# Moving a head pair's transposes to token rows one query tile later, and an overflow list's constants behind the routing

## The chip, the cores and the metric

The kernel runs on one core of a Trainium2 chip. A core has five engines that each work through their own list of instructions in order: TensorE (PE in the profile; its weight loads are shown as PEld), VectorE (DVE), ScalarE (ACT), GpSimd (POOL) and SyncE (SP), which here only issues DMA transfers. Matrix products go to PSUM, a small memory that VectorE and ScalarE empty into SBUF, the working memory. The metric is the device time of one execution in microseconds; less is better.

## The reference, cut to what matters

Three parts follow each other. All sizes: 4 batches, 8 heads, 576 tokens, head width 64, model width 512.

```
# 1: attention with a decay from a running sum of s, per batch and head
cum = cumsum(max(s, 0)); bias = min(-(cum[i] - cum[j]), 0)
attn = softmax(q @ k.T / 8 + bias, causal) @ v
x = attn, the 8 heads side by side              # [4, 576, 512]
# 2: a gated dense layer per batch
h = gelu(x @ w_in); u, v = halves of h; v = layernorm(v) * g_ln
v = w_sg @ v (over tokens) + b_sg; x2 = x + (u * v) @ w_out
# 3: a mixture of 8 experts, one expert per token
logits = x2 @ w_gate; local = sigmoid(x2 @ w_local)
e = argmax(logits) where local < 0.5 or at a batch's first token, else the token before's e
out = softmax(logits)[e] * relu(x2 @ w1[e]) @ w2[e]
```

## The kernel before, in words

Nearly every product is made of two or three matmuls on a high part and a low part of its operands (fp32r), so most tiles exist as a pair such as xh and xl.

**Attention.** Heads are taken in order, two to a pair; a pair's 2 x 64 output rows fill the 128 partitions of one tile xf, which has two buffers. A head's queries are cut into five tiles of 128 (the last has 64). For each query tile: a score product (emit_R in batch 1, L496; emit_S, L871), the row's extreme on VectorE (L439), the exponential on ScalarE (L446), its scaling on GpSimd (L450), then transposes of the probabilities (emit_T: L531, copied by L539 and L540). Products with V (emit_PV, L570) come in two parts: the first 256 queries (u = 0) and the other 320 (u = 1). From head 12 on their result is copied by ScalarE (L579) and added by VectorE into xf (L580); before that ScalarE alone writes xf (L582).

**A finished pair.** emit_X(p) does two things with xf. GpSimd splits it into xh and xl (L593, L594), the columns that the dense layer multiplies. TensorE turns it into token rows with five transposes (L599), ScalarE copies these into a staging tile stg (L600, L601; one buffer), and two DMA stores write them to xtok_d in DRAM, from where the output products of the same batch read them back much later.

**Order.** A_steps is a generator: it emits attention work and yields an estimate of its cost. In batch 1 the order is a list (AFTER), run by R_steps and after. In batches 2 to 4 the scores run ahead of the rest by a few query tiles, and after_S does what follows a score: the transposes of its probabilities, after tile 2 the head's product with V for u = 0, after tile 1 the head before's product for u = 1 and, if that head closed a pair, emit_X. merge mixes these steps with those of the dense layer (M_steps) by the yielded costs, until a batch's four pairs are done; take(A, 7) then mixes seven attention steps with the output products of the batch before (O_steps). What is emitted is not yet the order on the engines: a planner, which simulates the engines with durations of its own, draws instructions forward when it believes that their engine would stand idle, and the resulting order of each engine is fixed before the kernel runs. All plain DMAs share SP's one queue, which works in order.

**Routing and overflow.** After a batch's dense layer, route finds each token's expert and its slot. Per token tile VectorE makes three operands from constants (l at L1106, aa at L1108 twice; three buffers each) and TensorE multiplies them into a slot table (L1112). VectorE ends it at L1114 and L1115 (the last entry of dmarks). In the last batch the first layer of expert 0 is already running on TensorE; its sections 0 and 3 are queued behind named routing products (EM). L1241 makes the low part of an expert's weights, once on GpSimd, otherwise on VectorE. emit_olist, emitted in the middle of the experts, builds a list of overflowing blocks; its constants are three rows of numbers from GpSimd (li), cast by VectorE to lf (L1149), and two copies cx (L1151, L1152). behind(x, name) puts x later than the named instruction on the same engine.

Of the kernel before, what the change touches and what calls it, by code (L numbers as in the profile page):

```python
# [24 lines left out]
def f32v(ap):  # L25
    return ap.bitcast(F32)
# [7 lines left out]
def kernel(  # L34
# [19 lines left out]
    PE, ACT, DVE, POOL, SP = nc.tensor, nc.scalar, nc.vector, nc.gpsimd, nc.sync  # L54
# [10 lines left out]
    KD = DM // 128  # L65
# [519 lines left out]
    F4, TA = 8, (1, 3)  # L585

    def emit_X(p):
        b, kt = divmod(p, KD)
        xf = XF.pop(p)
        xh = T(xp, [128, S], F32R, "xh", bufs=6)  # L590
        xl = T(xp, [128, S], F32R, "xl", bufs=6)
        XH[p], XL[p] = xh, xl
        POOL.tensor_scalar(out=xh, in0=xf, scalar1=1.0, scalar2=1.0, op0=ALU.mult, op1=ALU.mult)  # L593
        POOL.tensor_tensor(out=xl, in0=xf, in1=f32v(xh), op=ALU.subtract)  # L594
        pt, pt2 = ps(), ps()
        stg = T(ap_, [128, NQ, 128], F32, "stg")
        for i in range(NQ):
            dst = pt[0:QM[i], 128 * i:128 * i + 128] if i < 4 else pt2[0:QM[i], 0:128]
            PE.transpose(dst, xf[:, 128 * i:128 * i + QM[i]], ident)  # L599
        ACT.copy(out=stg[:, 0:4, :], in_=pt.rearrange("p (i d) -> p i d", d=128))  # L600
        ACT.copy(out=stg[0:QM[4], 4, :], in_=pt2[0:QM[4], 0:128])  # L601
        r0 = b * S
        dma(xtok_d[r0:r0 + 512, 128 * kt:128 * kt + 128].rearrange("(i p) d -> p i d", p=128), stg[:, 0:4, :])
        dma(xtok_d[r0 + 512:r0 + S, 128 * kt:128 * kt + 128], stg[0:QM[4], 4, :])
# [51 lines left out]
    def A_steps(LAG):  # L656
        yield from R_steps()
        fifo = []
        for g in range(2 * PR, NH):
            p, r = divmod(g, 2)  # L660
            for o, i in enumerate((0, 1, 2, 3) if r else (0, 1, 2, 4, 3)):
                if o == 0:
                    for x in when:
                        if when[x] == g:
                            prep_asm(x)
                    if not r:
                        tail_queries(p)
                        prep_cum(p)
                emit_S(g, i) if i < NQ - 1 else emit_tail(p)
                yield 2 * max(107, (128 * i + QM[i]) * 0.42)  # L670
                fifo.append((g, i))
                if r and i == 1:
                    fifo.append((g, NQ - 1))
                if (r, i) in PT2 and p + 1 < NP:
                    prep_T(p + 1, PT2.index((r, i)))
                    if (r, i) == PT2[1] and p + 2 < NP:
                        prep_load(p + 2)
                    yield 600
                for _ in range(LO):
                    if left:  # L680
                        yield from after(*left.pop(0))
                while not left and len(fifo) > LAG:
                    yield from after_S(*fifo.pop(0))
        for x in fifo:
            yield from after_S(*x)
        emit_PV(NH - 1, 1)
        yield 1230
        emit_X(NP - 1)
        done_x[0] += 1
        yield 600  # L690

# [3 lines left out]
    def after_S(g, i):  # L695
        emit_T(g, i)
        yield 110 * (i + 1)
        if i == 2:
            emit_PV(g, 0)
            yield 860  # L700
        if i == 1 and g > 2 * PR:
            emit_PV(g - 1, 1)
            yield 1230
            if g % 2 == 0:
                emit_X((g - 1) // 2)
                done_x[0] += 1
                yield 600
        if i == 1 and g + 2 < NH:
            prep_V(g + 2)

# [5 lines left out]
        (6, ("T04", "P10")),  # L716
        (7, ("P01", "T12", "T13", "V0")),
        (8, ("T14",)),
        (9, ("P11", "V1", "X")),
    ]  # L720

    def after(p, x):
        if x == "X":
            emit_X(p)
            done_x[0] += 1
            yield 600
            return
        g = 2 * p + int(x[1])
        if x[0] == "T":
            emit_T(g, int(x[2]))  # L730
            yield 110 * (int(x[2]) + 1)
        elif x[0] == "P":
            emit_PV(g, int(x[2]))
            yield (860, 1230)[int(x[2])]
        elif g + 2 < NH:
            prep_V(g + 2)
# [400 lines left out]
    def emit_olist(pool, after):  # L1137

        nb = NBLK - CAP
        dma(ids_d, ids)  # L1140
        li = T(pool, [1, 384], I32, "li")
        lf = T(pool, [1, 384], F32, "lf")
        r = T(pool, [128, 48], F32, "ol")
        x = POOL.iota(li[0:1, 0:NL], pattern=[[0, E], [128, nb]], base=128 * CAP, channel_multiplier=0)
        behind(x, after)
        POOL.iota(li[0:1, 128:128 + NL], pattern=[[1, E], [0, nb]], base=0, channel_multiplier=0)
        POOL.iota(li[0:1, 256:256 + NL], pattern=[[NBLK, E], [1, nb]], base=CAP, channel_multiplier=0)
        for a in range(3):
            DVE.tensor_copy(out=lf[0:1, 128 * a:128 * a + NL], in_=li[0:1, 128 * a:128 * a + NL])  # L1149
        cx = T(pool, [128, 2, E, nb], BF16, "cx")  # L1150
        behind(DVE.tensor_copy(out=cx[:, 0], in_=carry.unsqueeze(2).to_broadcast([128, E, nb])), dmarks[-1].ins.name)  # L1151
        DVE.tensor_copy(out=cx[:, 1], in_=pad.unsqueeze(2).to_broadcast([128, E, nb]))  # L1152
        p1 = rs()
        for a in range(3):
            PE.matmul(p1[0:NL, a:a + 1], lhsT=lf[0:1, 128 * a:128 * a + NL], rhs=ident[0:1, 0:1], start=True, stop=True)
        for z in range(2):
            PE.matmul(p1[0:NL, 3:4], lhsT=cx[:, z].rearrange("p e b -> p (e b)"), rhs=onesb[:, 0:1], start=(z == 0), stop=(z == 1))
        DVE.tensor_copy(out=r[0:NL, 0:4], in_=p1[0:NL, 0:4])
        fb = T(pool, [128, 1], BF16, "fb")
        DVE.tensor_tensor(out=r[0:NL, 4:5], in0=r[0:NL, 3:4], in1=r[0:NL, 0:1], op=ALU.is_gt)  # L1160
        DVE.tensor_copy(out=fb[0:NL], in_=r[0:NL, 4:5])
        p2 = rs()
        PE.matmul(p2[0:NL, 0:1], lhsT=ltri[0:NL, 0:NL], rhs=fb[0:NL], start=True, stop=True)
        DVE.tensor_copy(out=r[0:NL, 5:6], in_=p2[0:NL, 0:1])
        DVE.tensor_scalar(out=r[0:NL, 16:16 + NOV], in0=io128[0:NL, 0:NOV], scalar1=r[0:NL, 5:6], scalar2=r[0:NL, 4:5], op0=ALU.is_equal, op1=ALU.mult)
        p3 = rs()
        for a in range(2):
            PE.matmul(p3[0:1, NOV * a:NOV * a + NOV], lhsT=r[0:NL, 1 + a:2 + a], rhs=r[0:NL, 16:16 + NOV], start=True, stop=True)
        PE.matmul(p3[0:1, 2 * NOV:2 * NOV + 1], lhsT=fb[0:NL], rhs=onesb[0:NL, 0:1], start=True, stop=True)
        DVE.tensor_copy(out=olist, in_=p3[0:1, 0:2 * NOV + 1])  # L1170
# [372 lines left out]
```

## Time and profile before

| | |
|---|---|
| median of 3 runs | 828.35 us (828.02 to 830.55) |
| the profiled execution | 832.37 us |
| its span, first to last instruction | 830.1 us |
| TensorE matmuls in flight | 785.8 us, 95% |
| TensorE weight loads | 675.5 us, 81% |
| VectorE, ScalarE, GpSimd busy | 510.2, 436.0, 337.4 us |
| mean granted TensorE clock | 0.985 |

The profile is of one execution. A row of its timeline gives the start and length in us, the engine, the line of the kernel, the operation, written tile <- read tiles, the shape and the number of instructions merged in the row; in square brackets stands how long the engine stood idle before the row and what ended that. A row's length runs from its first instruction's start to its last one's end, and instructions of one engine can overlap by some tens of ns.

### The profile page before, as it was taken

The page shows a single profiled execution, that of the slowest core. Times are in us where ns is not written, and L with a number is a line of the kernel's source. Part 1 is how long each engine was busy: PE and PEld are TensorE (multiplying, and loading weights), DVE is VectorE, ACT ScalarE, POOL GpSimd, SP SyncE. Part 2 cuts the span into 40 slices and gives each one's busy share as a digit, 9 for nine tenths or more (in the row PEclk, how much of TensorE's full clock was granted, in tenths as well). Part 3 has the DMA queues.
Part 4 walks back from the last instruction along what each step waited for, and adds up shares of the span by engine and source line. Part 5 has one row for each costly group of instructions (what it writes and reads, how often), then busy time and mean ns, then how long its engine had stood idle before and what let it go on. Part 6 is the DMA issues. An engine that isn't in the chain of part 4 may idle for free. (4 is left out here: it accounts for less than half of the span.)

```text
span 830.1 us, 14670 instructions
## 1 busy us (share of the span) xinstructions
PE 785.8 (95%) x4832; PEld 675.5 (81%) x4832; DVE 510.2 (61%) x1469; ACT 436.0 (53%) x1040; POOL 337.4 (41%) x614
## 2 busy tenths in 40 slices
PE   9887989899999999999999999989999999999995
PEld 5565877698789799789797778778988989899894
DVE  6787567685776789676884577664644445443420
ACT  6776567675547786246873254144544444444410
POOL 6787436575625578325684010060031220313101
PEclk9999999999999999989999999999999999999998
DMA  8568599845787575768442842153664444635401
GB/s 189 140 188 229 145 267 263 216 145 119 159 254 200 121 219 128 193 199 197 97 155 79 279 143 109 58 191 128 164 212 144 137 165 129 200 113 174 128 4 36
DMA packets 118041, 133.06 MB, mean 160 GB/s; under 512 B 69603, under 2 KB 83043, under 8 KB 117963
## 3 DMA queue, kind: packets, MB, share of 16 engines
q1 hardware_dynamic: 114123, 122.61, 53.6%
q0 software_dynamic: 3840, 9.48, 3.2%
q8 instruction: 40, 0.66, 0.3%
q14 instruction: 38, 0.31, 0.1%
HBM read 90.99 MB, written 22.95 MB: 137 GB/s over the span
## 5 line engine op out<-in xcount | busy, mean ns | idle before, releaser
L1241 DVE TENSOR_TENSOR wp<-wraw,wp 128x1024 fp32r<-128x1024 f32 x63 | 76.6, 1224 | 95.8 <-ACT wp L1240 91.3
L871 PE MATMUL ps<-wp,hT 128*128 128x512 f32 x528 | 123.0, 392 | 0.0
L871 PE MATMUL ps<-xT,wp 128*128 128x384 f32 x672 | 119.1, 336 | 0.0
L871 PEld LDWEIGHTS ps<-xT,wp 128*128 128x128 f32 x672 | 117.3, 188 | 0.7
L871 PEld LDWEIGHTS ps<-wp,hT 128*128 128x128 f32 x528 | 98.6, 188 | 21.1
L1297 POOL DMA_INDIRECT out_dram<-y,ids x24 | 29.4, 1224 | 212.3 <-ACT y L1296 175.0
L1240 ACT CAST wp<-wraw 128x1024 fp32r<-128x1024 f32 x64 | 66.5, 1049 | 62.6 <-DMA wraw<-in_moe_w_dram 56.0
L446 ACT ACTIVATE E<-E,negm 128x128 f32<-128x128 f32 (+4 forms) x136 | 79.4, 585 | 34.3 <-DVE negm L439 30.6
L450 POOL TENSOR_SCALAR E<-E,lsum 128x128 f32<-128x128 f32 (+4 forms) x136 | 77.8, 575 | 37.1 <-DVE lsum L448 28.3
L570 PE MATMUL ps<-et,vv 128*128 128x320 f32 (+9 forms) x476 | 82.5, 314 | 8.5 <-DVE et L537 5.2
L570 PEld LDWEIGHTS ps<-et,vv 128*128 128x128 f32 (+1 forms) x476 | 65.7, 173 | 22.8 <-DVE et L537 6.2
L439 DVE CUSTOM_DVE_ANT_0 E<-ps,zmask 128x128 f32<-128x128 f32 (+4 forms) x136 | 63.5, 471 | 17.9 <-PE ps L871 14.6
L447 POOL TENSOR_SCALAR lsum<-lsum 128x1 f32<-128x1 f32 (+1 forms) x128 | 31.2, 244 | 104.6 <-ACT E L446 88.3
L531 PE MATMUL ps<-ident,E 128*128 128x128 f32 (+1 forms) x452 | 67.6, 262 | 4.6 <-POOL E L450 1.6
L539 ACT CAST et<-ps 128x384 fp32r<-128x384 f32 (+3 forms) x120 | 50.2, 427 | 37.2 <-PE ps L531 35.3
L871 PE MATMUL ps<-wsg,vg 128*128 128x288 f32 x448 | 67.7, 302 | 0.8 <-DVE g L880 0.8
L871 PE MATMUL ps<-xh,w 128*128 128x288 f32 x256 | 59.3, 309 | 4.6 <-DVE wsg L857 2.9
L871 PEld LDWEIGHTS ps<-wsg,vg 128*128 128x128 f32 x448 | 62.0, 191 | 1.4 <-DVE g L880 1.0
L531 PEld LDWEIGHTS ps<-ident,E 128*128 128x128 f32 (+1 forms) x452 | 47.4, 140 | 16.5 <-issue 4.6
L540 DVE TENSOR_TENSOR et<-ps,et 128x384 fp32r<-128x384 f32 (+3 forms) x120 | 57.0, 481 | 4.6 <-ACT et L539 4.1
L871 PE MATMUL ps<-w,vg 128*128 128x512 f32 (+1 forms) x216 | 55.4, 400 | 0.0
L1285 DVE SCALAR_TENSOR_TENSOR hT<-ps,hT 128x384 fp32r<-128x384 f32 x56 | 30.3, 554 | 40.2 <-ACT hT L1284 40.0
(312 smaller groups left out, 1569.9 us busy)
## 6 DMA issues: line engine op xcount, KB each, us to landing
wraw<-in_moe_w_dram SPq DMA_DIRECT2D x64, 512.0 KB
qk<-qk SPq DMA_DIRECT2D x24, 432.0 KB
w<-wv_d SPq DMA_DIRECT2D x16, 512.0 KB
w<-wo_d SPq DMA_DIRECT2D x16, 512.0 KB
qk<-qk SPq DMA_DIRECT2D x24, 288.0 KB
w<-wu_d SPq DMA_DIRECT2D x12, 512.0 KB
nq<-in_q_dram SPq DMA_DIRECT2D x30, 144.0 KB
nk<-in_k_dram SPq DMA_DIRECT2D x30, 144.0 KB
```

Of the source, the lines that this page charges most:

```text
L439: hred[g] = DVE.tensor_tensor_reduce(out=e[:, a:z], in0=pt[:, 0:z - a], in1=zmask[:, m0:m0 + z - a], scale=-1.0, scalar=BIG if hi == 0 els ...
L446: ACT.activation(out=x, in_=x, func=ACTF.Exp, scale=-1.0, bias=nm, accum_out=l[:, z:z + 1])
L447: POOL.tensor_scalar(out=l, in0=l, scalar1=1e-9, scalar2=0.0, op0=ALU.add, op1=ALU.add)
L450: POOL.tensor_scalar(out=x, in0=x, scalar1=l[:, z:z + 1], scalar2=1.0, op0=ALU.mult, op1=ALU.mult)
L531: PE.transpose(pt[:, j * M:(j + 1) * M], e[h, 128 * j:128 * (j + 1)], ident[h, h])
L539: ACT.copy(out=dst[0], in_=src)
L540: DVE.tensor_tensor(out=dst[1], in0=src, in1=f32v(dst[0]), op=ALU.subtract)
L570: PE.matmul(x, lhsT=l, rhs=rhs if g >= F4 else f32v(rhs), start=(j == 0 and n_ == 0), stop=(j == js[-1] and n_ == len(ms) - 1),)
L871: ms = [PE.matmul(pt, lhsT=l, rhs=r, start=(first_ and x == 0), stop=(last_ and x == n - 1)) for x, (l, r) in enumerate(pairs)]
L1240: c = ACT.copy(out=w[:, 0, :], in_=r)
L1241: a = (POOL if (e, j) == (0, KD) else DVE).tensor_tensor(out=w[:, 1, :], in0=r, in1=f32v(w[:, 0, :]), op=ALU.subtract)
L1285: DVE.scalar_tensor_tensor(out=ht[:, 1, f, 0:w_], in0=pt[:, 0:w_], scalar=0.0, in1=f32v(ht[:, 0, f, 0:w_]), op0=ALU.max, op1=ALU.subtract)
```

## The change

In batches 2 to 4 the second half of emit_X (transposes, copies, stores) becomes a step of its own, emit_Y, which is emitted one query tile later: after the next head's tile 2 and its product with V for u = 0. In batch 1 X and Y follow each other in the list as before, but as two entries; the entries of pair 3 that are left over are worked off three to a step, so its Y comes one step later. The last pair's Y follows its X directly. The yields are divided into 50 and 550. In emit_olist, the three casts and the second copy on VectorE are put behind the last routing instruction.

```diff
--- before.py
+++ after.py
@@ -585,13 +585,16 @@
     F4, TA = 8, (1, 3)
 
     def emit_X(p):
-        b, kt = divmod(p, KD)
-        xf = XF.pop(p)
+        xf = XF[p]
         xh = T(xp, [128, S], F32R, "xh", bufs=6)
         xl = T(xp, [128, S], F32R, "xl", bufs=6)
         XH[p], XL[p] = xh, xl
         POOL.tensor_scalar(out=xh, in0=xf, scalar1=1.0, scalar2=1.0, op0=ALU.mult, op1=ALU.mult)
         POOL.tensor_tensor(out=xl, in0=xf, in1=f32v(xh), op=ALU.subtract)
+
+    def emit_Y(p):
+        b, kt = divmod(p, KD)
+        xf = XF.pop(p)
         pt, pt2 = ps(), ps()
         stg = T(ap_, [128, NQ, 128], F32, "stg")
         for i in range(NQ):
@@ -686,6 +689,7 @@
         emit_PV(NH - 1, 1)
         yield 1230
         emit_X(NP - 1)
+        emit_Y(NP - 1)
         done_x[0] += 1
         yield 600
 
@@ -698,13 +702,16 @@
         if i == 2:
             emit_PV(g, 0)
             yield 860
+            if g % 2 == 0 and g > 2 * PR:
+                emit_Y((g - 1) // 2)
+                yield 550
         if i == 1 and g > 2 * PR:
             emit_PV(g - 1, 1)
             yield 1230
             if g % 2 == 0:
                 emit_X((g - 1) // 2)
                 done_x[0] += 1
-                yield 600
+                yield 50
         if i == 1 and g + 2 < NH:
             prep_V(g + 2)
 
@@ -716,14 +723,18 @@
         (6, ("T04", "P10")),
         (7, ("P01", "T12", "T13", "V0")),
         (8, ("T14",)),
-        (9, ("P11", "V1", "X")),
+        (9, ("P11", "V1", "X", "Y")),
     ]
 
     def after(p, x):
         if x == "X":
             emit_X(p)
             done_x[0] += 1
-            yield 600
+            yield 50
+            return
+        if x == "Y":
+            emit_Y(p)
+            yield 550
             return
         g = 2 * p + int(x[1])
         if x[0] == "T":
@@ -1146,10 +1157,10 @@
         POOL.iota(li[0:1, 128:128 + NL], pattern=[[1, E], [0, nb]], base=0, channel_multiplier=0)
         POOL.iota(li[0:1, 256:256 + NL], pattern=[[NBLK, E], [1, nb]], base=CAP, channel_multiplier=0)
         for a in range(3):
-            DVE.tensor_copy(out=lf[0:1, 128 * a:128 * a + NL], in_=li[0:1, 128 * a:128 * a + NL])
+            behind(DVE.tensor_copy(out=lf[0:1, 128 * a:128 * a + NL], in_=li[0:1, 128 * a:128 * a + NL]), dmarks[-1].ins.name)
         cx = T(pool, [128, 2, E, nb], BF16, "cx")
         behind(DVE.tensor_copy(out=cx[:, 0], in_=carry.unsqueeze(2).to_broadcast([128, E, nb])), dmarks[-1].ins.name)
-        DVE.tensor_copy(out=cx[:, 1], in_=pad.unsqueeze(2).to_broadcast([128, E, nb]))
+        behind(DVE.tensor_copy(out=cx[:, 1], in_=pad.unsqueeze(2).to_broadcast([128, E, nb])), dmarks[-1].ins.name)
         p1 = rs()
         for a in range(3):
             PE.matmul(p1[0:NL, a:a + 1], lhsT=lf[0:1, 128 * a:128 * a + NL], rhs=ident[0:1, 0:1], start=True, stop=True)
```

## Rows read from the trace of the kernel before

**Rows 1.** Busy time by stretch: stretch, length, each engine's busy us, clock, DMA share, GB/s

```profile
366.00:450.00 84.00, 80.34 (x568) 72.54 (x568) 62.49 (x194) 57.97 (x156) 52.69 (x103) 0.99 0.46 120
530.00:545.00 15.00, 11.97 (x79) 8.87 (x78) 10.97 (x47) 2.93 (x5) 3.10 (x3) 1.00 0.20 62
545.00:830.00 285.00, 275.45 (x1441) 249.19 (x1440) 119.24 (x164) 116.16 (x179) 58.11 (x49) 0.99 0.44 139
```

**Rows 2.** TensorE's waits: line, waited for, us in total, times, longest

```profile
PE rt L1112 <- DVE aa L1108: 3.6, 3, 2.7
PE ps L599 <- DVE xf L580: 3.6, 4, 1.3
```

**Rows 3.** Timeline of TensorE at pair 9, and at the last pair

```profile
283.87 0.44 PE L599 MATMUL ps<-ident,xf 128*128 128x128 f32 x2
285.06 0.55 PE L599 MATMUL ps<-ident,xf 128*128 128x128 f32 x3 [0.76 <-DVE xf L580]
285.36 0.49 PE L871 MATMUL ps<-qk 128*128 128x256 f32 x2
285.69 0.49 PE L531 MATMUL ps<-ident,E 128*128 128x128 f32 x3
285.94 0.65 PE L570 MATMUL ps<-et,vv 128*128 128x256 f32 x4
...
447.49 0.55 PE L599 MATMUL ps<-ident,xf 128*128 128x128 f32 x3 [1.28 <-DVE xf L580]
```

**Rows 4.** Timeline of ScalarE, VectorE and GpSimd at pair 9

```profile
284.07 0.42 ACT L579 COPY xc<-ps 64x320 f32<-64x320 f32 x1 [0.65 <-PE ps L570]
...
284.52 0.48 DVE L580 TENSOR_TENSOR xf<-ps,xc 64x320 f32<-64x320 f32 x1 [0.38 <-ACT xc L579]
...
283.41 1.05 POOL L450 TENSOR_SCALAR E<-E,lsum 128x512 f32<-128x512 f32 x2
```

**Rows 5.** Timeline of TensorE in the last batch's routing

```profile
540.53 0.54 PE L1112 MATMUL rt<-aa,l 128*128 128x288 bf16 x3
543.76 0.28 PE L1112 MATMUL rt<-aa,l 128*128 128x288 bf16 x1 [2.69 <-DVE aa L1108]
544.38 0.28 PE L1112 MATMUL rt<-aa,l 64*128 64x288 bf16 x1 [0.34 <-DVE aa L1108]
```

**Rows 6.** Timeline of VectorE and GpSimd in the same stretch

```profile
540.46 0.22 DVE L1152 COPY cx<-pad 128x120 bf16<-128x120 bf16 x1
540.59 2.51 DVE L1149 CAST lf<-li 1x120 f32<-1x120 int32 x2
543.02 0.24 DVE L1106 TENSOR_SCALAR l<-io,cf 128x128 bf16<-128x128 bf16 x1
...
540.30 2.58 POOL L1241 TENSOR_TENSOR wp<-wraw,wp 128x1024 fp32r<-128x1024 f32 x1 [0.47 <-ACT wp L1240]
```

**Rows 7.** Lines 1149 and 1108: ns shortest/median/longest, first and last start

```profile
L1149 DVE CAST lf<-li x3: 201/203/2375, 540.6 to 652.4; 1x120 f32<-1x120 int32 x3
...
L1108 DVE TENSOR_SCALAR aa<-ioc,cf,wtok x40: 299/314/757, 234.0 to 544.0; 128x144 bf16<-128x144 bf16 x40
```

**Rows 8.** Lines 600 and 601, the copies into stg, likewise

```profile
L600 ACT COPY stg<-ps x16: 571/586/590, 40.0 to 448.0; 128x512 f32<-128x512 f32 x16
...
L601 ACT COPY stg<-ps x16: 258/259/268, 40.5 to 448.4; 64x128 f32<-64x128 f32 x16
```

**Rows 9.** Timeline of SP's DMA queue at pair 9

```profile
286.15 0.95 SPq L78 DMA_DIRECT2D xtok_d<-stg  x2
287.19 0.56 SPq L78 DMA_DIRECT2D vr<-in_v_dram  x1
```

**Rows 10.** Timeline of VectorE and GpSimd in batch 2's routing

```profile
361.47 1.03 DVE L1108 TENSOR_SCALAR aa<-ioc,cf,wtok 128x144 bf16<-128x144 bf16 x2
...
361.45 0.72 POOL L429 TENSOR_TENSOR vv<-vr,vv 128x256 fp32r<-128x256 f32 x1
```

**Rows 11.** Busy time by stretch behind the routing, columns as in rows 1

```profile
544.00:548.00 4.00, 3.67 (x20) 3.48 (x20) 3.20 (x9) 1.00 (x2) 2.17 (x2) 0.66 0.44 151
```

## Prediction

> **What bounds the kernel now.** I read the busy time by stretch first [rows 1]. TensorE has matmuls in flight for 80.34 of 84 us where attention and the dense layers run interleaved (366 to 450) and for 275.45 of 285 us in the expert part; VectorE, ScalarE and GpSimd have a quarter or more of those stretches free. So an edit pays only where it takes a wait off TensorE, and a wait taken off another engine is worth nothing by itself. One stretch differs: from 530 to 545, the routing of the last batch, TensorE has only 11.97 of 15 us.
>
> Next I read who made TensorE wait [rows 2]. Two rows belong to this change. The products of the slot table (line 1112) waited 3.6 us in three waits for VectorE, the longest 2.7. The transposes to token rows (line 599) waited 3.6 us in four waits for VectorE's last addition into xf, the longest 1.3. The rest of TensorE's 44 us of idle time (830.1 less 785.8) lies on lines that are not touched. So the direct stake is about 7 us of 830.
>
> Then I read both places in order of time. At pair 9 [rows 3] two transposes, which need only the part of xf that was finished earlier, follow the last product with V at once; the other three start at 285.06, after 0.76 us of nothing. The reason is in the other engines' rows [rows 4]: ScalarE's copy of the product's lower half starts at 284.07 and takes 0.42, VectorE's addition starts at 284.52 and takes 0.48, so xf is complete at 285.00. This in-order wait is what moving the transposes can take away. It is rarer than the code suggests: 16 pairs run the same code, four waits of this kind are recorded [rows 2]. Of their 3.6 us, the 1.28 before 447.49 is the last pair's [rows 3]; the other three (pairs 6, 9 and 13) share 2.3, 0.76 or 0.77 each. At the remaining pairs other matmuls stood in front of the transposes.
>
> At the routing [rows 5, 6], TensorE starts three table products at 540.53, then waits 2.69 for the fourth and 0.34 for the fifth. Between the operands of the third token tile and those of the fourth, VectorE ran one copy for the overflow list (540.46) and two casts of 120 numbers on one partition, 2.51 together. Such a cast takes 201 ns at its fastest and 2375 ns here [rows 7].
>
> **The token rows, part by part.** No instruction is added or removed: per pair five transposes, two copies of 586 and 259 ns [rows 8] and two stores, in another place. The split on GpSimd into xh and xl stays where it was. Eleven pairs (4 to 14) move behind the next head's product with V for its first 256 queries; pair 3 moves by one query tile; pairs 0 to 2 and the last keep their order, so the last pair's 1.28 us stays.
>
> At pair 9 the score matmul (285.36), the transposes of the probabilities (285.69) and four value products (285.94) would come first [rows 3]. They need nothing of xf; GpSimd's scaling of probabilities, two in 1.05 from 283.41, is over at 284.46 [rows 4]. They would fill TensorE from about 284.3 to 285.3, and xf is done at 285.00, before its transposes come up. So a wait of 0.76 goes. From start to start it is a little more: transposes follow each other at 0.14 ((0.55 less 0.27 for one) over two), so the third could have started at 283.87 + 2 x 0.14 = 284.15 and started at 285.06, 0.9 later. Three pairs give 3 x 0.76 = 2.3, at most 3 x 0.9 = 2.7. I take 2.3, the idle time that the rows show. For the other eight pairs I count nothing: no wait is recorded there now.
>
> Cost of the move: the two copies, 0.845 us on ScalarE, now stand among the exponentials and probability copies of the next head. Their cover is ScalarE's free time, 26 of 84 us in the stretch to 450 [rows 1]. With the cover gone each of the 11 pairs would cost up to 0.845, 9.3 in all; I take 0 and keep 9.3 as the far end. The stores go through SP's one queue, in order: at pair 9 it issued them from 286.15 in 0.95 us, with a load of a coming V at 287.19 right behind [rows 9]. After the change that load is ahead of them, and nobody waits for a token row before the output products of its batch, a whole stretch later. I take 0; were a load of V late by a store's wait, it would have a head's time in hand. xf has two buffers, and the one of pair p is written again only for pair p+2, so no wait comes from there. In the two stretches where seven attention steps are mixed with an output product, the moved transposes are now one of the seven, and one step of the next head slides into the following stretch. That costs nothing as long as TensorE bounds both.
>
> **The overflow constants.** The casts and the copy may now start only behind the finished slot table. One cast already ran at 652 us [rows 7]. Gone from the routing are the copy and two casts. Read naively this returns the 2.2 us (2375 less 201 ns) that the first cast lost. But why did it take 2375 ns? GpSimd ran a subtraction over 128x1024 from 540.30 for 2.58, to 542.88 [rows 6], and the cast, from 540.59, is over at 542.96, just behind it. The table's own operands are VectorE instructions of one input from SBUF as well: at 361.47 one of line 1108 took 757 ns against a median of 314, and a GpSimd subtraction ran from 361.45 to 362.17 [rows 7, 10]. So whatever of this kind stands next in VectorE's queue stays until GpSimd is done, and after the change that is the operand itself (line 1106, which ran at 543.02 [rows 6]). Having three buffers, it also waits for the first table product, which starts at 540.53 [rows 5], behind GpSimd's start. Then the operand ends at about 542.96, where the first cast ended, and its successor starts where the second cast did, at about 542.9 instead of 543.2: 0.3 us gained. The two ends are therefore 0.3 if the operand is held and 2.2 if it is not. I take 0.3, the row of 757 ns being the nearest.
>
> The Trainium skill's page "SBUF — State Buffer" (section "Who interferes with whom") says that VectorE's copies, casts and tensor_scalar operations in a two-port form and GpSimd's operations hold one pair of ports in turn, the later one blocked until the earlier ends. By that rule the operands are blocked as the casts were, and the term is 0.3; without it, 2.2. The 757 ns agree with the rule; that line 1106 itself is blocked no row here shows.
>
> The moved casts land behind 545, where VectorE is busy for 119 of 285 us [rows 1]; should GpSimd hold one again for 2.2, the evictions queued behind it are late by that, which the seven PSUM buffers cover (without them, TensorE waits those 2.2).
>
> **Sum.** 2.3 + 0.3 = 2.6. The profiled execution took 832.37 (span 830.10 and 2.27 around it), so it would take 829.8. It lies 4.0 above the median of the runs; the same difference from 828.35 gives 825.7. With one of the three pairs not repaid it is 1.8, with the start-to-start figure 3.0: the likeliest case's own range is 825.3 to 826.6.
>
> **Rivals.**
> *The routing is freed entirely.* If VectorE's operands pass GpSimd, the routing returns 2.2, and perhaps the clock as well: behind the two waits the granted clock was 0.66 from 544 to 548 [rows 11], part of the time at 1.2 instead of 2.4 GHz, a loss of 4 x 0.34 = 1.4. With the pairs 2.3 + 2.2 + 1.4 = 5.9, so 822.4. For it: nothing but the casts is seen to be held for so long. Against: the 757 ns. Chance 0.15.
>
> *Nothing comes of it.* The wait moves: TensorE reaches the next tile's probabilities 0.76 earlier and waits there for GpSimd or ScalarE, and the routing is held by GpSimd. Gain 0 to 0.5, so 828.1. For it: the slack at pair 9 is thin (probabilities done at 284.46, wanted at about 284.5). Against: only matmuls that are ready stand ahead at pair 9. Chance 0.22.
>
> *Slower: the copies on ScalarE.* Each pair's 0.845 us in front of a next head's exponential or probability copy delays the chain that TensorE waits for. At 6 of 11 pairs it costs 5.1 less the 2.6, 2.5 slower, and from there it decides; at all 11, 9.3 less 2.6 = 6.7. So 830.9 to 835.1. For it: ScalarE is busy for 58 of 84 us there and works in order, and the planner that fixes that order works from its own durations. Against: 26 us are free, and a copy does not wait for xf any more when it comes up. Chance 0.21.
>
> The forecast has the remaining 0.42.
>
> **How the numbers follow.** Runs of this kernel can tell about 0.3%, 2.5 us, from no change. The forecast's 2.6 lies on that bound: I give 0.24 of its 0.42 to faster and 0.18 to no change. Faster: 0.24 + 0.15 + 0.03 of the second rival = 0.42. No change: 0.18 + 0.19 = 0.37. Slower: the third rival, 0.21. The range from 821.5 to 832 leaves out the edge of the freed routing (0.05) and the upper half of the slower case (0.1).
>
> **What would show it.** In the profile after: no wait of line 599 on xf at pairs 6, 9 and 13, and the last pair's still there; the copies of line 600 amid the next head's work; no casts between the table's operands, but one operand of some 2.3 us there while GpSimd subtracts, and TensorE's wait for line 1112 still above 2. The prediction is wrong if that wait falls below 1, if the waits of lines 531 or 570 grow by more than 2 us, or if the order, which is planned anew for the whole kernel, opens a wait of the routing's size at a place that the change does not name.

## The result, and the profile after

The changed kernel takes 821.55 us (median of 19 runs, 815.12 to 829.23) against 830.55 for the kernel before in the same rounds (19 runs, 822.5 to 841.34). The ratio is 0.99, with a 95% interval of 0.9877 to 0.9923: faster by 1.0%, 8.3 us of 830. The forecast was 825.7 with a range of 821.5 to 832. The direction is right and the time is inside the range by 0.05 us, but the gain is some three times the 2.6 us of the sum. That the time is inside is luck: the forecast started from 828.35, and a ratio of 0.99 on that would be 820.1, below the range.

The first lines of the page of the profiled execution after (its time is 822.43, its span 820.6):

```profile
span 820.6 us, 14652 instructions
PE 784.2 (96%) x4832; PEld 674.7 (82%) x4832; DVE 513.1 (63%) x1469; ACT 436.0 (53%) x1040; POOL 334.8 (41%) x614
```

TensorE still has nearly the same work, 784.2 us against 785.8. What went is its idle time: 820.6 less 784.2 is 36.4, where it was 44.3. The kernel is bound as it was, and in these two profiles 7.9 of the 9.5 us by which the spans differ are idle time of TensorE. The waits of TensorE that answer to [rows 2]:

```profile
PE rt L1123 <- DVE aa L1119: 3.1, 4, 2.3
PE ps L602 <- DVE xf L580: 1.3, 1, 1.3
```

Line 1112 is now line 1123, and 599 is 602. Of the four waits for VectorE's xf one is left, 2.3 us are gone. Two more waits of the transposes, 0.40 and 0.95 us at pairs 0 and 1, are for the xf that ScalarE writes there (line 582). They stand in both profiles, and the change keeps the order of these two pairs; the prediction, which says that at the remaining pairs other matmuls stood in front, overlooked them. The timeline of TensorE at pairs 6, 9 and 13 and at the last pair, which answers to [rows 3], shows which:

```profile
196.12 0.73 PE L602 MATMUL ps<-ident,xf 128*128 128x128 f32 x5
...
282.74 0.45 PE L570 MATMUL ps<-et,vv 128*128 128x256 f32 x3
283.03 0.73 PE L602 MATMUL ps<-ident,xf 128*128 128x128 f32 x5
...
398.31 0.73 PE L602 MATMUL ps<-ident,xf 128*128 128x128 f32 x5
...
438.11 0.55 PE L602 MATMUL ps<-ident,xf 128*128 128x128 f32 x3 [1.28 <-DVE xf L580]
```

At pairs 6, 9 and 13 the five transposes are one row of 0.73 us with no bracket behind it. Value products of the next head stand in front of them. The last pair, whose order was kept, still waits its 1.28. The copies into stg now stand amid the next head's work on ScalarE, between its copy of a value product (579) and its copies and exponentials of the probabilities (539, 446):

```profile
283.59 0.37 ACT L579 COPY xc<-ps 64x256 f32<-64x256 f32 x1
283.99 0.59 ACT L603 COPY stg<-ps 128x512 f32<-128x512 f32 x1
284.47 0.26 ACT L604 COPY stg<-ps 64x128 f32<-64x128 f32 x1
284.63 0.43 ACT L539 CAST et<-ps 128x320 fp32r<-128x320 f32 x1
```

They take 0.59 and 0.26, as before [rows 8], and TensorE does not wait longer for the probabilities than before: its waits of line 570 for VectorE's copies (537) are 4.9 us after and 5.2 before, those of line 531 for GpSimd's scaling 1.7 and 1.6.

The timelines of TensorE, VectorE and GpSimd in the last batch's routing answer to [rows 5, 6]:

```profile
531.51 0.54 PE L1123 MATMUL rt<-aa,l 128*128 128x288 bf16 x3
534.31 0.28 PE L1123 MATMUL rt<-aa,l 128*128 128x288 bf16 x1 [2.26 <-DVE aa L1119]
534.93 0.28 PE L1123 MATMUL rt<-aa,l 64*128 64x288 bf16 x1 [0.34 <-DVE aa L1119]
...
530.82 0.25 DVE L1117 TENSOR_SCALAR l<-io,cf 128x128 bf16<-128x128 bf16 x1
531.84 1.96 DVE L1117 TENSOR_SCALAR l<-io,cf 128x128 bf16<-128x128 bf16 x1 [0.33 <-PE rt L1123]
537.20 0.34 DVE L1160 CAST lf<-li 1x120 f32<-1x120 int32 x2
...
531.39 2.36 POOL L1252 TENSOR_TENSOR wp<-wraw,wp 128x1024 fp32r<-128x1024 f32 x1 [0.50 <-ACT wp L1251]
```

The casts have left the routing (two run at 537.20, in 0.34 together). In their place the operand of line 1117 takes 1.96 us, where the same instruction took 0.25 a microsecond earlier. It ends at 533.80, just behind GpSimd's subtraction (531.39 + 2.36 = 533.75). TensorE's waits for operands in the routing go from 2.69 + 0.34 to 2.26 + 0.34.

So both places that the change names behave as forecast, and they give 2.3 + 0.4 us. The profiled spans differ by 9.5. The table of stretches tells where the rest is. It is cut at the same instructions in both kernels: the start of the transposes of pair 2, the end of the product that ranks each batch's tokens (the last with tile u), the last table product, the last matmul. Columns are stretch, length, busy time of TensorE, its weight loads, VectorE, ScalarE, GpSimd, granted clock, DMA share, GB/s. Before:

```profile
76.90:215.90 139.00, 127.80 (x888) 110.68 (x887) 89.11 (x289) 89.06 (x248) 80.06 (x161) 0.96 0.74 193
215.90:333.50 117.60, 115.18 (x809) 102.37 (x808) 92.74 (x324) 78.22 (x218) 70.75 (x153) 1.00 0.70 181
333.50:456.00 122.50, 116.82 (x766) 101.94 (x765) 86.10 (x284) 68.52 (x185) 63.10 (x125) 0.97 0.56 152
...
527.60:544.70 17.10, 14.07 (x86) 10.52 (x87) 12.93 (x58) 3.17 (x6) 3.10 (x3) 1.00 0.19 60
544.70:820.50 275.80, 275.75 (x1442) 249.49 (x1442) 119.54 (x165) 115.47 (x178) 57.13 (x48) 0.99 0.46 143
```

And after:

```profile
78.40:211.40 133.00, 125.68 (x884) 109.75 (x882) 88.99 (x286) 89.09 (x248) 79.20 (x160) 0.95 0.77 201
211.40:327.90 116.50, 115.86 (x812) 103.21 (x812) 94.44 (x326) 77.74 (x218) 70.33 (x152) 1.00 0.71 183
327.90:446.70 118.80, 115.04 (x766) 100.19 (x765) 87.62 (x284) 68.48 (x184) 63.68 (x126) 1.00 0.60 157
...
518.60:535.20 16.60, 14.01 (x86) 10.46 (x86) 12.13 (x55) 3.17 (x6) 2.83 (x3) 1.00 0.18 55
535.20:811.00 275.80, 275.80 (x1443) 249.54 (x1442) 120.05 (x169) 115.31 (x178) 55.78 (x48) 0.99 0.45 144
```

Read the lengths in pairs. Up to pair 2 the order is the same, and after is 1.5 longer there (78.4 to 76.9). The second stretch, with pair 9, is 1.1 shorter and the routing 0.5: what was priced. The expert part has the same 275.80. The third lost 3.7, and the first lost 6.0, though of the waits that the change aims at only pair 6's 0.76 lies in it. The surplus sits there, and the experiments had to tell which of it is the change's.

### The profile page after: what moved, and what is told of

The parts are those of the page before. It is cut to its first block, busy times and chain, and to the rows that moved or that the text cites. A ratio compares the mean times of both kernels' runs of the same rounds, so it can differ in the third digit from the quotient of the medians.

```text
span 820.6 us, 14652 instructions
## 1 busy us (share of the span) xinstructions
PE 784.2 (96%) x4832; PEld 674.7 (82%) x4832; DVE 513.1 (63%) x1469; ACT 436.0 (53%) x1040; POOL 334.8 (41%) x614
```

## The experiments

In what follows a version's "net length" is the time from pair 2's transposes to the last table product with each stretch multiplied by its granted clock. It takes off most of what a stretch at the lower clock level costs in one profiled execution and not in the next. It is worked out from tables like the two above, so it is an estimate. How good it is can be seen up to pair 2, where TensorE's order is the same in all versions: lengths of 76.9, 80.7 and 86.0 us there (before, "constants only", "pair 3 alone") become 76.9, 75.9 and 75.7. It takes off about 1 us too much where the clock was low for long; so lengths as they stand are given beside it where a reading rests on it. Before it is 133.4 + 117.6 + 118.8 + 71.6 + 17.1 = 458.5, and after 126.3 + 116.5 + 118.8 + 71.9 + 16.6 = 450.1: 8.4 less, as much as the runs measure. Each ratio below is to the kernel before in the same rounds, with its 95% interval.

| version | ratio | net length | of it in the first stretch |
|---|---|---|---|
| before | 1 | 458.5 | 133.4 |
| constants only | 1.0012 (0.9978 to 1.0045) | 458.3 | 133.2 |
| the change | 0.9900 (0.9877 to 0.9923) | 450.1 | 126.3 |
| the change, run again | 0.9871 (0.981 to 0.9932) | 450.3 | 127.4 |
| token rows only | 0.9937 (0.9905 to 0.9969) | 449.5 | 126.8 |
| change, eight steps taken | 0.9935 (0.99 to 0.997) | 450.3 | 127.1 |
| accounting only | 0.9972 (0.9943 to 1.0001) | 457.9 | 129.0 |
| move only | 0.9978 (0.9946 to 1.0009) | 457.1 | 132.5 |
| move, 600 and 0 | 0.9931 (0.9902 to 0.996) | 456.6 | 130.3 |
| pairs 3 to 7 | 0.9967 (0.9928 to 1.0006) | 455.6 | 127.2 |
| pairs 8 to 14 | 0.9952 (0.9912 to 0.9992) | 457.6 | 134.2 |
| pair 3 alone | 0.9918 (0.9891 to 0.9945) | 453.1 | 127.1 |
| pairs 4 to 14 | 0.9944 (0.9909 to 0.9979) | 454.7 | 131.1 |
| subtraction on VectorE | 0.9885 (0.982 to 0.995) | 448.3 | 127.7 |

### The two halves apart

Token rows only: the change, with the four constants back where they were.

```diff
-            behind(DVE.tensor_copy(out=lf[...], in_=li[...]), dmarks[-1].ins.name)
+            DVE.tensor_copy(out=lf[...], in_=li[...])
-        behind(DVE.tensor_copy(out=cx[:, 1], ...), dmarks[-1].ins.name)
+        DVE.tensor_copy(out=cx[:, 1], ...)
```

> The token rows moved as in the change, the overflow constants left where they were; TensorE, ScalarE, GpSimd and SP run exactly the changed kernel's order, VectorE all but five instructions of it. If the constants are worth what the profiles show at the routing (waits of line 1112 there 3.03 us before, 2.60 after), this kernel is 0.4 us slower than the full change, ratio to before about 0.990 to 0.991, and the 2.4 us cast is back between the operands. If the constants carry a large part (2.2 us and 1.4 us of clock), the ratio is 0.994 or more.

Measured: 823.84 against 827.83. On TensorE, ScalarE, GpSimd and SP the order is that of the change, and only rows of VectorE differ. The casts are back in the routing and the wait there is again 2.69 + 0.22, against 2.26 + 0.34 in the change. The net length is that of the change. The ratio, 0.9937, lies between what was expected with the constants worth little (0.990 to 0.991) and with a large part (0.994 or more), and its interval reaches into both. So most of the gain belongs to the token rows; whether the constants have a part is seen in the next run.

Constants only: the kernel before, with the opposite edit.

```diff
-            DVE.tensor_copy(out=lf[...], in_=li[...])
+            behind(DVE.tensor_copy(out=lf[...], in_=li[...]), dmarks[-1].ins.name)
-        DVE.tensor_copy(out=cx[:, 1], ...)
+        behind(DVE.tensor_copy(out=cx[:, 1], ...), dmarks[-1].ins.name)
```

> Only the overflow constants behind the routing, the token rows as before. TensorE, ScalarE, GpSimd and SP run exactly the order of the kernel before, VectorE all but these few rows. Theory held operand: line 1106 takes about 2 us under GpSimd's subtraction, the waits of the table products fall from 3.03 to about 2.6 us, the ratio is 0.999 to 1.000. Rival (the casts alone were late): the waits fall below 1, ratio 0.996.

Measured: 828.95 against 829.23, no difference. In the routing the waits are 1.83, 0.33 and 0.33, 2.5 us in all against 3.0 before. Here it is the third tile's operands of line 1108 that are held: the two take 2.73 us from 535.97, beside GpSimd's subtraction from 536.29 for 2.35. TensorE, ScalarE, GpSimd and SP have exactly the order of the kernel before here, which makes its table a second profiled execution of that order. Its first and third stretch:

```profile
80.70:215.20 134.50, 125.26 (x888) 108.22 (x886) 89.25 (x289) 89.02 (x248) 80.20 (x161) 0.99 0.76 199
332.80:452.50 119.70, 114.81 (x766) 99.81 (x765) 85.85 (x284) 67.74 (x184) 63.12 (x125) 1.00 0.57 155
```

The third stretch takes 119.70 at clock 1.00, where the profile of before had 122.50 at 0.97. So of the 3.7 us by which the change seemed shorter there, 2.8 belong to that one execution of the kernel before: a wait of 1.43 us at 359.58 for VectorE's g and a clock of 0.57 from 360 to 368. Neither is in this run. What remains is 119.7 to 118.8, 0.9: pair 13's wait. The net length of the first stretch, on the other hand, is the same in both executions (133.2 and 133.4), and the change takes 6 to 7 off it. TensorE's order in that stretch is one and the same in three of the versions (before, "constants only", "pairs 8 to 14") and in six others (the change twice, "token rows only", "eight steps taken", "pairs 3 to 7", "subtraction on VectorE"). Without the clock taken off, the three take 139.0, 134.5 and 136.9 us there and the six 130.6 to 133.0: 5.1 less on average.

### The routing: who holds the operand

The change, with the one subtraction that GpSimd does for the first expert's weights given to VectorE.

```diff
-        a = (POOL if (e, j) == (0, KD) else DVE).tensor_tensor(out=w[:, 1, :], in0=r, in1=f32v(w[:, 0, :]), op=ALU.subtract)
-        if (0, KD) < (e, j) < (1, KD):
+        a = DVE.tensor_tensor(out=w[:, 1, :], in0=r, in1=f32v(w[:, 0, :]), op=ALU.subtract)
+        if (0, KD) <= (e, j) < (1, KD):
```

> The changed kernel, but the low part of expert 0's first second-layer weights is made by VectorE behind the finished slot table instead of by GpSimd in the middle of the routing. Theory held operand (line 1117 took 1.96 us because GpSimd's subtraction of 2.36 was running): the operand takes 0.25, TensorE's wait for the fourth table product falls from 2.26 below 0.5, the routing is 1.7 to 2.2 us shorter, the low clock behind it may go too (1.7 more), ratio to before 0.986 to 0.988. Rival (the operand waits for something else, such as the weights' transfer or a buffer): the wait stays above 1.5 and the ratio is that of the change.

Measured: 820.08, ratio 0.9885; the change in the same rounds 819.46 and 0.9871. TensorE and VectorE in the routing:

```profile
531.74 0.28 PE L1123 MATMUL rt<-aa,l 128*128 128x288 bf16 x1 [0.55 <-DVE aa L1119]
...
530.98 0.25 DVE L1117 TENSOR_SCALAR l<-io,cf 128x128 bf16<-128x128 bf16 x1 [0.32 <-PE rt L1123]
533.49 2.36 DVE L1252 TENSOR_TENSOR wp<-wraw,wp 128x1024 fp32r<-128x1024 f32 x2
```

Without GpSimd at work the operand takes its 0.25 again, and the wait of 2.28 that the change has there in the same rounds falls to 0.55. The clock behind it stays up as well: 1.00 from 533 to 537, where the change has 0.57. That settles what holds the operand.

The Trainium skill's page "SBUF — State Buffer" (section "Who interferes with whom") says that GpSimd and a VectorE tensor_scalar in a two-port form hold a shared pair of ports in turn, the later one blocked until the earlier is done. The trace agrees with that rule: 1.96 us beside GpSimd and 0.25 without it.

Whether this version is faster the runs cannot tell: their intervals are 0.6% to either side, some 5 us. The timeline of TensorE tells what became of the gain. This version:

```profile
530.65 0.54 PE L1123 MATMUL rt<-aa,l 128*128 128x288 bf16 x3
...
557.90 1.47 PE L1282 MATMUL ps<-ident,xg 128*128 128x128 f32 x12
559.86 0.73 PE L882 MATMUL ps<-wp,hT 128*128 128x512 f32 x2 [0.49 <-ACT hT L1357]
561.24 3.03 PE L882 MATMUL ps<-wp,hT 128*128 128x512 f32 x12 [0.64 <-DVE hT L1358]
564.10 0.33 PE L882 MATMUL ps<-xT,wp 128*128 128x384 f32 x1
```

And the change in the same rounds:

```profile
529.14 0.54 PE L1123 MATMUL rt<-aa,l 128*128 128x288 bf16 x3
531.95 0.28 PE L1123 MATMUL rt<-aa,l 128*128 128x288 bf16 x1 [2.28 <-DVE aa L1119]
...
559.64 1.47 PE L1282 MATMUL ps<-ident,xg 128*128 128x128 f32 x12
560.87 3.44 PE L882 MATMUL ps<-wp,hT 128*128 128x512 f32 x14
564.15 0.33 PE L882 MATMUL ps<-xT,wp 128*128 128x384 f32 x1
```

This version comes to the routing 1.51 us behind (530.65 to 529.14), because the stretch before it ran at a clock of 0.98 in this execution and at 1.00 in the other. The shorter wait puts it 0.21 ahead (531.74 to 531.95), and the higher clock 1.74 ahead at the transposes of xg (557.90 to 559.64). Then TensorE waits 0.49 and 0.64 for evictions of hT, and at 564.10 the lead is 0.05. In front of these evictions stands a weight tile: ScalarE's cast of it waited 0.31 for its transfer and ran at 558.28 for 1.05, and VectorE's part of it at 559.36 for 1.23. Both spans are 818.2. So of 3.3 us won, 1.7 by the wait and 1.5 by the clock behind it, about 1.7 are lost at hT. The other 1.5 stay, and equal spans hide them only because this execution came late to the routing. It is one execution each, and the ratios neither show nor exclude 1.5 us. The 0.4 of the constants is below what the runs can tell as well, as the run with the constants alone says.

### The move and its accounting

The change says two things to the planner: where the transposes go, and that a step with X takes 50 and one with Y 550 instead of 600 together. These versions take them apart, and try whether one step that slid over a border is what pays. First, everything as in the change, but eight attention steps mixed with an output product instead of seven.

```diff
-            merge(take(A, 7), O_steps(b), 7.0, O_COST)
+            merge(take(A, 8), O_steps(b), 7.0, O_COST)
```

> The full change with eight instead of seven attention steps mixed with each output product, so that these stretches hold the same attention work as before the change. Theory output stretch (the gain of 3.7 us between the second and third routing comes from one attention step sliding out of the stretch where TensorE waited 1.43 us at 359.6 for an output tile's addition): that wait and the low clock behind it return, ratio to before 0.994 or more. Theory merge (the gain is in the mixed stretches): ratio 0.989 to 0.991, as the change.

Measured: 822.92, net length 450.3, as the change, and the wait and the low clock in the third stretch did not come back (118.5 us at a clock of 1.00). The slid step is not the cause. The ratio, 0.9935, is that of "token rows only" in the same rounds.

Accounting only: Y's work done at the end of X, where it was before, with the separate steps kept and empty.

```diff
+        emit_Y0(p)     # at the end of emit_X
-    def emit_Y(p):
+    def emit_Y0(p):
...
+    def emit_Y(p):
+        pass
```

> The transposes, copies and stores stay directly behind the split into xh and xl, as before; only the accounting of the change is kept: 50 at X, and an empty step of 550 where Y would stand; constants as in the change. Theory moved transposes (the gain is the transposes' own place): the waits of line 599 on xf stay (about 2.3 us in three pairs) and the ratio is 0.997 to 1.003. Theory merge (the gain comes from the other interleaving of attention and dense layer that the new steps and yields bring): at least half of the gain without any moved transpose, ratio 0.990 to 0.995.

Measured: 825.74, 0.28% less. There are six waits for VectorE's xf, 4.7 us in all, two more than before. The first stretch is shorter by 4.4, but the second and the third are longer by 2.5 and 4.1; part of the 4.1 are five matmuls that stood in the fourth stretch before (771 against 766), which is 2.3 shorter.

Move only: the transposes moved as in the change, with 600 for X and no step of Y's own. That is so for pairs 4 to 14; pair 3 keeps its two entries in batch 1's list, with 50 and 550, here and in the version behind it.

```diff
-                yield 550
...
-                yield 50
+                yield 600
```

> The transposes, copies and stores moved as in the change for pairs 4 to 14, but with the old accounting: 600 at X and no step for Y, so the mixing counts as before the change; constants as in the change. Theory moved transposes: ratio 0.989 to 0.992, as the change. Theory merge: only the three pairs' waits and the constants are gained, 2.6 us, ratio 0.996 to 0.998.

Measured: 827.37, 0.22% less (1.8 us, near the 2.3 of the pairs, but the interval reaches to no change). Waits for VectorE's xf: the last pair's alone. But among TensorE's waits there is one of 2.1 for VectorE's g, and one that neither the kernel before nor the change has:

```profile
PE ps L881 <- POOL vg L946: 1.6, 1, 1.6
```

And with 600 for X and a step of its own at 0 for Y:

```diff
-                yield 550
+                yield 0
...
-                yield 50
+                yield 600
```

> The change with 600 charged at X and 0 at Y: Y stays a step of its own and counts among the seven, only the charge of 550 comes before the next head's tile instead of behind it. Theory charge (the charge of 550 behind the tile is what shifts the mixing): idle time as with the old accounting, about 22 us, the wait for the output tile's addition is back, ratio 0.996 to 0.998. Theory step (that Y is one of the seven steps): idle time 17 to 18.5 us, ratio 0.989 to 0.993.

Measured: 824.39, 0.69% less, net length 456.6. Only the last pair waits for VectorE's xf, and a wait for GpSimd's vg is there (1.59).

In all of these the waits for xf go or come as the mechanism says. What the version is worth beyond that does not follow them: the same move gives 0.2%, 0.7% or 1.0% with three sets of numbers for the planner, and the intervals of the first and the last do not meet.

### Which pairs

The change again, as it is, for comparison with the three versions of its rounds.

> The changed kernel once more, beside the parts of it on one chip. Both theories: ratio to before 0.988 to 0.992. Its profile against the first one tells how much of a stretch's length is the execution's own (clock, transfers): the order of every engine is the same, so the idle time of TensorE between the second pair's transposes and the last routing should again be near 14.7 us, against 21.9 before.

Measured: 819.46, ratio 0.9871; span 818.2, waits for xf 1.3.

Pairs 3 to 7 moved, the others as before:

```diff
-            if g % 2 == 0 and g > 2 * PR:
+            if g % 2 == 0 and g > 2 * PR and (g - 1) // 2 < 8:
...
+                if not ((g - 1) // 2 < 8):
+                    emit_Y((g - 1) // 2)
...
-                yield 50
+                yield 50 if (g - 1) // 2 < 8 else 600
```

> The change for pairs 3 to 7 alone (they stand in the first mixed stretch and the first output stretch); pairs 8 to 14 as before; constants as in the change. Theory first stretch (most of the gain, 7 us without the clock's share, lies between the second pair's transposes and the first routing): ratio 0.990 to 0.993. Theory pair by pair (0.76 us for each of pairs 6, 9 and 13): only pair 6 and the constants, 1.2 us, ratio 0.998 to 0.999.

Measured: 828.94 against 831.47, ratio 0.9967. Waits for VectorE's xf: 3.3 us in four, all at pairs that were not moved. The first stretch is as short as in the change (127.2), but the second and third are 3.3 and 1.4 longer than its 116.5 and 118.8.

Pairs 8 to 14 moved (the same test with `>= 8`, and pair 3 as before):

> The change for pairs 8 to 14 alone; pairs 3 to 7 as before; constants as in the change. Theory first stretch: what is left is the wait of 1.43 us at 359.6 with the low clock behind it and pairs 9 and 13, at most 5 us where both go, ratio 0.994 to 0.997. Theory pair by pair: 2 x 0.76 and the constants, ratio 0.997 to 0.998.

Measured: 827.3, ratio 0.9952. The first stretch, where nothing is moved, keeps the length of the kernel before (134.2), and pair 6 waits 1.12. The second and third are as short as in the change.

Pair 3 alone (the test with `< 4`):

> Only pair 3's transposes stand one query tile later, as a step of their own in batch 1's list; pairs 4 to 14 as before; constants as in the change. Theory of many small waits (TensorE's idle time between pair 2's transposes and the last routing, 25.0 us before and 16.7 to 17.3 with the change, is made of many places, and each new order of the planner changes several of them): the first mixed stretch loses 1 to 2 us of idle time at the wait of line 857, the three waits on xf stay, ratio 0.996 to 0.999. Theory first stretch (its gain comes from the start of the mixing, which pair 3's move shifts): idle time 20 us or less, ratio 0.993 or less.

Measured: 822.04 against 829.23, ratio 0.9918. Of the two theories on record, the one of many small waits expected 0.996 to 0.999 and missed; the other expected 0.993 or less, and that came. Its profiled execution took 831.32, 9.3 us more than the median; 9.1 of that it lost before pair 2, at a low clock (86.0 us, where before took 76.9), so only the stretches behind are read. Pair 9 keeps its wait, on TensorE's timeline:

```profile
286.87 0.33 PE L602 MATMUL ps<-ident,xf 128*128 128x128 f32 x1 [0.76 <-DVE xf L580]
```

Pair 13 keeps its wait too. The change is 3.0 shorter than this in net length, 1.8 of it in the second stretch and 0.8 in the third, where those two waits lie. The rest of the change's gain is here already, in the first stretch (127.1), with one pair of twelve moved: and pair 3 waited for nothing before.

All but pair 3 (pairs 4 to 14):

```diff
-        (9, ("P11", "V1", "X", "Y")),
+        (9, ("P11", "V1", "X")),
...
+            emit_Y(p)
-            yield 50
+            yield 600
```

> The change without pair 3: its transposes stay with the split; pairs 4 to 14 moved with the new steps and yields; constants as in the change. Theory of many small waits: idle time of TensorE 17 to 19 us, ratio 0.990 to 0.993. Theory first stretch (pair 3's move matters): idle time above 20 us, ratio 0.995 or more.

Measured: 825.62, ratio 0.9944, between the two theories' ranges (0.990 to 0.993, and 0.995 or more). Waits for VectorE's xf: the last pair's alone. The first stretch is 131.1 net, 2.3 less than before; but it had a clock of 1.00 throughout, and as it stands it is as long as the change's own 130.6 to 133.0. So this run does not show that the first stretch needs pair 3's move. The third is that of the change (118.6), but the second is 117.6, that of the kernel before, though pair 9's wait is gone.

## Why the prediction was right, and why its size was not

**The transposes** were right in mechanism and size. 2.3 us of waiting for xf are gone, at the three pairs named, and the last pair's 1.28 stays. In "pair 3 alone", where pairs 9 and 13 are not moved, their 0.76 is still there. The third stretch gives 0.9 for pair 13 (119.7 to 118.8), which is the start-to-start figure. The second gives 1.1, but not by pair 9 alone: TensorE's idle time there falls from 2.4 to 0.6, and four matmuls more lie in it.

**The moved copies** cost nothing that shows: 0.59 and 0.26 us inside ScalarE's free time, with the waits of lines 531 and 570 as before. The rival of the late copies on ScalarE, 830.9 to 835.1, is refuted, and by the same rows the one in which the wait only moves. Nor do the stores show as holding up a load: TensorE's only wait for a load of V is one of 2.1 us in the profiles of both kernels.

**The constants** were right in mechanism and near in size: the operand itself is held, 0.4 us instead of 0.3, and not the 2.2 of the free routing. Giving the subtraction to VectorE shows that GpSimd holds it. The rival of the freed routing, 822.4, came near the result, but not by its mechanism. With the operand freed by that edit, the routing and the clock behind it gave 1.7 + 1.5 us, where the rival had 2.2 + 1.4; what it lacked is that about half is lost again at the evictions of hT.

**The step that failed** is the one that took the rest of TensorE's idle time as lying "on lines that are not touched", and with it the count of nothing for pair 3 and the eight pairs without a wait. The lines are not touched, but the order is: it is planned anew for the whole kernel from the emitted steps and their accounts. Compared place by place in the two traces, with line numbers left out, another instruction stands at about 1160 of TensorE's 4832 places, 700 of VectorE's 1469, 490 of ScalarE's 1040 and 270 of GpSimd's 614. The prediction named this as a way to be wrong, but only as a wait that opens and without a price. Here it closed some. TensorE's waits from 76.9 to 215.9 before:

```profile
PE ps L871 <- DVE wsg L857: 2.9, 1, 2.9
PE ps L570 <- DMA vv<-in_v_dram: 2.1, 1, 2.1
PE ps L871 <- DVE negm L439: 1.2, 2, 1.0
PE ps L599 <- DVE xf L580: 0.8, 1, 0.8
```

The same order once more ("constants only", 80.7 to 215.2):

```profile
PE ps L871 <- DVE wsg L857: 1.4, 1, 1.4
PE ps L871 <- DVE negm L439: 1.2, 2, 1.0
PE ps L599 <- DVE xf L580: 1.1, 1, 1.1
```

And from 78.4 to 211.4 after:

```profile
PE ps L570 <- DMA vv<-in_v_dram: 2.1, 1, 2.1
PE ps L882 <- DVE wsg L868: 1.7, 1, 1.7
PE ps L570 <- DVE et L540: 0.8, 1, 0.8
PE ps L882 <- DVE qk L382: 0.7, 1, 0.7
```

The wait for wsg differs as much between two executions of one order (2.9 and 1.4) as between the kernels, so nothing is read from it. Line 871's for negm, 1.2 in both, and xf's are gone; 0.7 for qk and 0.8 for et are new. TensorE's idle time in the stretch is 11.2, 9.2 and 10.0 in three executions of the order before and 7.3 to 9.0 in six of the other, 2.2 less on average. None of these tiles but xf is in the diff.

**What the size is made of.** From the table: 8.4 us of net length, of which 2.3 to 2.7 are the three pairs, 0.4 is the routing, and about 5 to 6 lie in the first stretch, by another order there; by lengths as they stand it is about 4 there. That the edit to pair 3 does not make them by itself is shown by pairs of versions. Moving pair 3, which waited for nothing, takes 6.3 off that stretch. Moving it in the same way, with other accounts for the pairs behind it, takes 0.9 ("move only") or 3.1 (600 and 0). Not moving anything but changing the accounts takes 4.4 ("accounting only"). By lengths as they stand, against 136.8 on average for the order before, the four take 5.8, 3.1, 1.2 and 6.5. Where both move and accounts there are those of the kernel before ("pairs 8 to 14", "constants only"), TensorE's order there is that of before, and nothing is taken off. The kernel before had one of the worst orders of that stretch among those run, and that the change happened on one of the best is luck.

**What stays open** is which decision of the planner it is. No single ingredient carries it. Nor is the whole length accounted for: it fell by 5.1 on average, the idle time by 2.2. Four matmuls, three of 288 columns and one transpose, slid over the border into the second stretch (888 before, 884 after), about half a us. The rest is time in which TensorE counts as busy with the same matmuls. Part may be of the kind seen at pair 9, where five transposes are in flight for 0.44 + 0.55 in two pieces before and for 0.73 in one after; that was not followed up. The intervals are 0.2 to 0.7% wide to either side, so neighbours in the table, such as the change and "pair 3 alone", are not told apart by their times.

No version beats the change by more than the runs can tell; the one with the subtraction on VectorE cannot be told from it.

## What to carry to other kernels

A wait that is seen in the trace can be priced well from its rows, but in a kernel whose order is planned by a program a local edit is also a new draw of the whole order, here worth about twice the edit: give that draw a term of its own, and a range to both sides. Before such an edit is credited with a gain, try the same edit with other accounts for the planner and the accounts without the edit, and look for the stretch in which the gain sits. And take two profiles of the same order before reading a wait in one of them as the kernel's: one of 1.43 us, and the low clock behind it, was only that execution's. The same holds for equal spans: compare two versions by the lead at single instructions, because a late start in one of them can hide what an edit gave.

## What the runs showed of the hardware

The granted clock of one and the same order differs from execution to execution by about what the change is worth. From 8 to 28 us it was 1.00 in the profile of before and 0.75 in that of "constants only", which has the same order on TensorE; that is half the time at 1.2 instead of 2.4 GHz, and pair 2's transposes started at 80.7 instead of 76.9. In "pair 3 alone", whose TensorE order up to there is the same too, it was 0.50 over the whole of that stretch, and they started at 86.0:

```profile
8.00:28.00 20.00, 20.00 (x77) 12.27 (x76) 9.30 (x32) 8.79 (x27) 5.45 (x20) 0.50 0.75 171
```

TensorE counts as busy for all 20.00 us there with 77 matmuls, where before has 126 in 18.39. A busy share near one is therefore no sign that TensorE does much: the clock column has to be read beside it. The times scatter likewise (815 to 829 us for the changed kernel), and the ratios here are known to 0.2% at best.
